# Three edits at the start of a recurrent-attention kernel: V stores behind the Wo load, the first Wq quarter in two pieces, and the order of the second half's context matmuls

## The chip, the cores and the metric

The program runs on 1 core of one Trainium2 chip. Its time is the device time of one execution in microseconds (us). Three runs of the kernel before gave 838.24, 837.37 and 839.92 us, so the median is 838.24 us. Lower is better.

## The reference, cut to what matters

Two layers on 2048 tokens of width 512, in bfloat16. Layer A is attention with a recurrent memory: the tokens are cut into 64 segments of 32; eight memory rows are put ahead of each segment, and the first eight rows of the segment's output are the next segment's memory, so the 64 steps can't run side by side. Layer B is a gated MLP that mixes over all tokens. Layer A takes most of the time, and the edits lie in its first steps and, for the matmul order, in each of them.

```
_A_ref(x, mem0, Wq, Wk, Wv, Wo):           # 32 heads of 128
    mem = mem0                              # 8 rows
    for s in range(64):
        h = concatenate([mem, x[32 rows of segment s]])        # 40 rows
        q, k, v = h @ Wq, h @ Wk, h @ Wv                       # per head
        p = softmax(mask(q @ k.T * scale))
        o = (p @ v) @ Wo                                       # summed over heads
        mem = o[:8];  outs.append(o[8:])
h  = x + _A_ref(_layernorm(x), ...)
h2 = h + _B_ref(_layernorm(h), ...)         # gelu, layernorm, w_sp mixing, w_out
```

## The kernel before, in words

**Tiles and stages.** All of Wq, Wk, Wv and Wo (4 MB each) stay on chip in one buffer, `f_arena`. The start loads them in quarters of 1 MB (eight heads) and meanwhile projects rows that don't depend on the memory: the last eight rows of each segment, transposed into `hTe` in four chunks of 16 segments (`ck`). Then come 64 steps `s`. A step projects 32 of its 40 rows (`QK`, line 539; `V_half`, line 645), multiplies queries by keys (`S_half`, lines 590 and 596), takes the softmax, multiplies by the values (`PV_half`, lines 670 and 676), evacuates that context to `cT` (lines 694 and 696), applies Wo (`Wo`, line 708) and makes the next memory (`mem_out`, line 735). Heads 0 to 15 are half `b = 0`, heads 16 to 31 half `b = 1`. In the gaps of a step stand matmuls that the chain doesn't need at once, among them V projections of later chunks (`vx_mm`, line 476).

**V projections of the extra rows.** `vx_mm(ck, n)` makes the `n`th of eight pieces of a chunk. `vx_evac` (lines 480 to 505) copies the piece from PSUM to a staging buffer and stores it to DRAM (`vext_d`, DMA issue on line 494), from where `load_vx` (line 511) fetches one segment's values. Chunk 0 is staged in `part`; other chunks go through the two halves of `Vs` in turn (`vcnt`), so an evacuation has to wait until the store that last read its half has landed. For chunk 0 and `n >= 2` the stores of the later segments are put off: `vrest[0]` holds six stores of segments 2 to 5, `vrest[1]` those of segments 6 to 15.

**Order.** `Emitter.add` lists instructions in program order, engine by engine, and derives the semaphore waits from the tokens read and written. Every engine runs its own list in order. SP and ACT issue DMAs in their lists, and an issue that has to wait holds up all that stands behind it. DMAs of SP and ACT take the semaphores `fdma0` to `fdma35` in turn.

**Around the change.** Wq's quarters come first, the upper two 128-row blocks of each on SP's queue and the lower two on ACT's (`load_w`, line 313). SP goes on with x, Wv, Wk and Wo (line 922). The start's Q and K groups of four heads (`qkx_full`, line 449) begin with heads 0 to 3. Step 0 makes pieces (1, 0) and (1, 1) of V in the middle, (1, 2) and (2, 0) behind its context; (2, 0) is evacuated by ACT (line 488) behind `mem_out`, ahead of ACT's mask copy (line 574) and ACT's evacuations of the next step's Q and K (line 550). Behind the evacuation of (1, 1), step 0 lists the six held `vrest[0]` stores with a wait for Wo's last quarter, a transposing read of `w_sp` (`wT_read(0, 0)`, line 851) and a load of x rows (`load_xe(3, 1)`, line 303).

**Context banks.** The four 32-row groups `c` of a half write four PSUM banks. For half 1 the order of `c` is 1, 2, 3, 0 in the first 16 matmuls and 2, 1, 3, 0 in the last four; the Wo matmuls and the evacuations go 0, 2, 1, 3.

Of the kernel before, what the change touches and what calls it, by code (L numbers as in the profile page):

```python
# [169 lines left out]
def fast_path(nc, st, keep, flags, A_x, A_mem0, A_Wq, A_Wk, A_Wv, A_Wo, A_seg_len, B_w_in, B_w_sp, B_b_sp, B_w_out, out):  # L170
# [3 lines left out]
    DH = A_Wq.shape[2]  # L174
# [21 lines left out]
    em = Emitter(n_dma_sems=40)  # L196

    def sb(name, shape, dt):
        return st.enter_context(nc.sbuf_tensor("f_" + name, shape, dt))
# [19 lines left out]
    hTe = sb("hTe", [128, NCK, DC, 128], BF)  # L219
# [12 lines left out]
    partx = sb("partx", [128, 512], BF)  # L232
# [38 lines left out]
    def PB(b):  # L271
        return ("ps", b)

    def sp(fn, **k):
        return em.add("sp", fn, dma=True, **k)

    def pe(fn, **k):
        return em.add("pe", fn, **k)

    def act(fn, **k):  # L280
        return em.add("act", fn, **k)

    def dve(fn, **k):
        return em.add("dve", fn, **k)
# [13 lines left out]
    def xbuf(j):  # L298
        return (xn[:, j, :], [("xn", j)]) if j < 2 else (part[:, j, :], [("part", j, 0), ("part", j, 1)])

    def load_xe(ck, j, queue="sp"):
        t, tok = xbuf(j)
        em.add(queue, lambda e: e.dma_start(t, xe[CK * ck:CK * ck + CK, XM:SEG, :]), dma=True, writes=tok)

    def load_w(mi, hq, queues=("sp",)):
        parts = len(queues)
        n = DC // parts
        wd, ws = ((A_Wq, w_q), (A_Wk, w_k), (A_Wv, w_v))[mi]
        wr = wd.rearrange("(dc p) h e -> p dc (h e)", p=128)
        cols = slice(hq * 8 * DH, (hq + 1) * 8 * DH)  # L310
        for k in range(parts):
            tok = ("W", mi, hq) if k == 0 else ("W", mi, hq, k)
            em.add(queues[k], lambda e, k=k: e.dma_start(ws[:, k * n:(k + 1) * n, cols], wr[:, k * n:(k + 1) * n, cols]), dma=True, writes=[tok])  # L313
            em.mark_const(tok)

    load_xe(0, 0)
    load_xe(1, 1, "act")
    for hq in range(4):
        load_w(0, hq, ("sp", "act"))
        if hq == 1:  # L320
            act(lambda e: e.preload_act_table_set("natural_log_exp_and_others"))
    load_x(0, 4)
# [120 lines left out]
    def qkx_full(ck, i, bank):  # L443
        mi, h0 = i // 8, 4 * (i % 8)
        ws = (w_q, w_k)[mi]
        for hh in range(4):
            h = h0 + hh
            for dc in range(DC):
                pe(lambda e, h=h, dc=dc, hh=hh: e.matmul(ps[:, bank, hh * 128:(hh + 1) * 128], lhsT=ws[:, dc, h * DH:(h + 1) * DH],
                                                         rhs=hTe[:, ck, dc, :], start=(dc == 0), stop=(dc == DC - 1)),  # L450
                   reads=[("hTe", ck), ("W", mi, h // 8) if mi or dc < 2 else ("W", mi, h // 8, 1)], writes=[PB(bank)])

    def qkx_full_evac(ck, i, bank, eng):
        mi, h0 = i // 8, 4 * (i % 8)
# [25 lines left out]
    def vx_evac(ck, n, bank, eng="act", queue="sp"):  # L480
        if ck == 0:
            t, tok = part[:, n, :], [("part", n, 0), ("part", n, 1)]
        else:
            j = vcnt[0] % 2
            vcnt[0] += 1
            t, tok = Vs[:, j, :], [("Vs", j)]
        if eng == "act":
            act(lambda e: e.activation(out=t, in_=ps[:, bank, :], func=ACT.Copy, scale=VSC), reads=[PB(bank)], writes=tok)
        else:
            dve(lambda e: e.tensor_scalar(out=t, in0=ps[:, bank, :], scalar1=VSC, scalar2=None, op0=ALU.mult), reads=[PB(bank)], writes=tok)  # L490
        def store(i0, i1, ks, queue="sp", after=()):
            r = slice(8 * i0, 8 * i1)
            dst = vext_d[ck, n, r, :, :].rearrange("p r e -> p (r e)")
            em.add(queue, lambda e: e.dma_start(dst, t[r, :]), dma=True, reads=tok, writes=[("vext", ck, n, k) for k in ks], after=after)

        if ck:
            store(0, CK, (0,), queue)
        else:
            store(0, 2, (0,), queue)
            if n < 2:  # L500
                store(2, CK, (1, 2))
            else:
                vrest[0].append(lambda after=(): store(2, 6, (1,), after=after))
                vrest[1].append(lambda: store(6, CK, (2,)))

    vcnt, vrest = [0], ([], [])
# [149 lines left out]
        else:  # L656
            dve(lambda e: e.tensor_scalar(out=dst, in0=src, scalar1=VSC, scalar2=None, op0=ALU.mult), reads=[PB(bank)], writes=tok)  # L657

    PVO = ((0, 1, 2, 3), (1, 2, 3, 0))

    def pv_bank(b, c):
        return CB if (b, c) == (1, 0) else PVB[c]

    def PV_half(s, b):
        xb = s % NVX
        for g in range(4):
            for c in PVO[b]:
                q = slice(32 * c, 32 * c + 32)
                c0 = 160 * b + 40 * g
                pe(lambda e, q=q, c=c, g=g, c0=c0: e.matmul(  # L670
                    ps[:, pv_bank(b, c), c0:c0 + 40], lhsT=V_sb[q, b, g * 128:(g + 1) * 128], rhs=E_sb[q, b, 0:160].rearrange("p (a g t) -> p a g t", a=5, t=8)[:, :, g, :],
                    start=(g == 0), stop=False, skip_group_check=True, tile_position=(32 * c, 0)),
                    reads=[("V", b, g), ("E", b)], writes=[PB(pv_bank(b, c))])
        for c in (PVO[0], (2, 1, 3, 0))[b]:
            q = slice(32 * c, 32 * c + 32)
            pe(lambda e, q=q, c=c: e.matmul(  # L676
                ps[:, pv_bank(b, c), 160 * b:160 * b + 160].rearrange("p (g q) -> p g q", q=40)[:, :, 0:16], lhsT=Vx[q, xb, b, :],
                rhs=E_sb[q, b, 160:224].rearrange("p (g q) -> p g q", q=16),
                start=False, stop=True, skip_group_check=True, tile_position=(32 * c, 0)),
                reads=[("Vx", xb), ("Ex", b)], writes=[PB(pv_bank(b, c))])  # L680
# [73 lines left out]
    def behind():  # L754
        return [em.by_eng["pe"][-1]]
# [93 lines left out]
    def wT_read(i, k):  # L849
        r = slice(8 * k, 8 * k + 8)  # L850
        sp(lambda e: e.dma_start_transpose(out=wst[:, r, :], in_=B_w_sp[i * 64:(i + 1) * 64, 1024 * k:1024 * k + 1024]),
           writes=[("wst", k)], after=behind())
# [36 lines left out]
    def start_x(ck, i):  # L889
        start_group(qkx_full, qkx_full_evac, ck, i)  # L890
# [5 lines left out]
    for hq in (0, 2, 1, 3):  # L896
        load_w(2, hq)
# [23 lines left out]
    for hq in range(4):  # L921
        sp(lambda e, hq=hq: e.dma_start(w_o[:, 8 * hq:8 * hq + 8, :], wor[:, 8 * hq:8 * hq + 8, :]), writes=[("Wo", hq)])  # L922
        em.mark_const(("Wo", hq))


    class Gap:
# [88 lines left out]
    for s in range(NSEG):  # L1015
# [3 lines left out]
            w2_load()  # L1019
        if j4 == 3 and rb > 0:  # L1020
            px_load(rb - 1)
        if s > 0:
            wT_read(s // 2, s % 2)

        def qk_piece(pi):
            QK(s, QKP[pi], range(2 if pi < 2 else 1 if pi == 2 and s else 0, DC))
# [67 lines left out]
        sm_rcp(1)  # L1094
        if s == 0:
            vx_evac(1, 1, 5, "act")
            for f in vrest[0]:
                f([em.last_w[("Wo", 3)]])
            wT_read(0, 0)
            load_xe(3, 1)  # L1100
        if s > 0:
            v_second()
        if j4 == 1:
# [210 lines left out]
    for i, rb in enumerate(order):  # L1314
# [8 lines left out]
        if i == 1:  # L1323
            pe(lambda e: e.matmul(ps[:, CB, :], lhsT=Sc[:], rhs=partx[:], start=True, stop=True),
               reads=["partx", "Sc"], writes=[PB(CB)])
# [52 lines left out]
    for tb in range(NTB):  # L1378
        for fb in range(len(ACC) if tb == 0 else 0, FB):
            bank = 5 + fb % 3 if tb == 0 else (tb * FB + fb) % 2  # L1380
# [777 lines left out]
```

## Time and profile before

| | us |
|---|---|
| median of three runs | 838.24 |
| the profiled execution, whole | 840.62 |
| its span, first to last instruction | 838.90 |
| TensorE (PE) busy in the span | 824.4 (98%) |
| ScalarE (ACT) busy | 514.2 (61%) |
| VectorE (DVE) busy | 475.9 (57%) |
| GpSimd (POOL) busy | 145.0 (17%) |

A span counts from the first instruction of the program to the last; the 1.72 us between it and the execution's time lie around it. All times inside a profile are from the span's start. PE is the matmul array, PEld its weight load, SPq the queue of SyncE, which issues most DMAs. A row of the timeline gives the start, the length, engine, source line, operation, output and inputs, and how many instructions are merged; brackets give the idle time before it and what ended that. A row of the waits gives the engine and line that waited, what released it, the total, the number of waits and the longest.

### The profile page before, as it was taken

The page shows a single profiled execution, that of the slowest core. Times are in us where ns is not written, and L with a number is a line of the kernel's source. Part 1 is how long each engine was busy: PE and PEld are TensorE (multiplying, and loading weights), DVE is VectorE, ACT ScalarE, POOL GpSimd, SP SyncE. Part 2 cuts the span into 40 slices and gives each one's busy share as a digit, 9 for nine tenths or more (in the row PEclk, how much of TensorE's full clock was granted, in tenths as well). Part 3 has the DMA queues.
Part 4 walks back from the last instruction along what each step waited for, and adds up shares of the span by engine and source line. Part 5 has one row for each costly group of instructions (what it writes and reads, how often), then busy time and mean ns, then how long its engine had stood idle before and what let it go on. Part 6 is the DMA issues. An engine that isn't in the chain of part 4 may idle for free.

```text
span 838.9 us, 48365 instructions
## 1 busy us (share of the span) xinstructions
PE 824.4 (98%) x21963; PEld 484.4 (58%) x21963; DVE 475.9 (57%) x1221; ACT 514.2 (61%) x1549; POOL 145.0 (17%) x412
## 2 busy tenths in 40 slices
PE   7999999999999999999999999999999999999998
PEld 7755565656566555655566656555665554444443
DVE  3546565656566555666556556565655576653344
ACT  2467777777777777777777777676666676300000
POOL 5202111121121111112211121111111123200000
PEclk9999999999999999999999999999999999999999
DMA  9975222122222222222212122333343278223101
GB/s 313 386 214 108 69 60 68 49 68 60 61 63 58 65 60 65 63 73 58 67 50 72 48 70 72 103 85 85 78 83 84 73 253 260 90 101 103 42 13 48
DMA packets 107652, 80.54 MB, mean 96 GB/s; under 512 B 49672, under 2 KB 97040, under 8 KB 107440
## 3 DMA queue, kind: packets, MB, share of 16 engines
q1 hardware_dynamic: 105712, 74.82, 30.8%
q8 instruction: 174, 2.85, 1.5%
q10 hardware_dynamic: 1504, 2.36, 0.9%
q14 instruction: 38, 0.31, 0.1%
q0 software_dynamic: 224, 0.20, 0.1%
HBM read 43.72 MB, written 23.13 MB: 80 GB/s over the span
## 4 chain that ended last, share of the span: by engine, by line
PE 92%; SPq 5%; DMA 1%; issue 0%; ACT 0%; DVE 0%; POOL 0%; POOLq 0%
PE f_ps L539 27%; PE f_ps L708 14%; PE f_ps L645 13%; PE f_ps L1266 12%; PE f_ps L426 4%; PE f_ps L764 4%; SPq L313 3%; PE f_ps L1360 3%; PE f_ps L1259 3%; PE f_ps L670 3%; PE f_ps L476 2%; PE f_ps L830 2%; PE f_ps L590 1%; DMA f_arena<-in_A_Wo_dram 1%; SPq L922 1%; PE f_ps L1226 1%
## 5 line engine op out<-in xcount | busy, mean ns | idle before, releaser
L539 PE MATMUL f_ps<-f_arena,f_hT 128*32 128x512 bf16 (+1 forms) x5120 | 238.5, 337 | 0.4
L539 PEld LDWEIGHTS f_ps<-f_arena,f_hT 128*32 128x32 bf16 x5120 | 124.4, 96 | 89.0 <-ACT f_hT L738 20.0
L550 ACT ACTIVATE f_Tst<-f_ps 128x512 bf16<-128x512 f32 (+2 forms) x320 | 143.4, 510 | 36.1 <-PE f_ps L539 28.5
L645 PE MATMUL f_ps<-f_arena,f_hT 128*32 128x512 bf16 x2048 | 139.8, 379 | 0.0
L708 PE MATMUL f_ps<-f_arena,f_cT 128*32 128x256 bf16 x4096 | 130.1, 273 | 2.2 <-DMA f_arena<-in_A_Wo_dram 1.3
L635 POOL TENSOR_TENSOR f_E_sb<-f_R_sb,f_E_sb 128x64 bf16<-128x64 f32 x128 | 47.5, 371 | 411.0 <-ACT f_R_sb L627 411.0
L708 PEld LDWEIGHTS f_ps<-f_arena,f_cT 128*32 128x32 bf16 x4096 | 97.0, 96 | 27.5 <-ACT f_cT L694 17.3
L558 DVE STREAM_TRANSPOSE f_QT<-f_Tst 128x256 uint32<-128x256 uint32 x128 | 57.1, 446 | 93.2 <-ACT f_Tst L550 93.2
L657 DVE TENSOR_SCALAR f_V_sb<-f_ps 128x512 bf16<-128x512 f32 (+1 forms) x128 | 71.4, 558 | 52.4 <-PE f_ps L645 52.4
L1266 PE MATMUL f_ps<-f_arena 128*128 128x512 bf16 x448 | 100.5, 379 | 0.0
L1266 PEld LDWEIGHTS f_ps<-f_arena 128*128 128x128 bf16 x448 | 43.7, 98 | 52.9 <-issue 0.3
L694 ACT ACTIVATE f_cT<-f_ps 128x160 bf16<-128x160 f32 (+1 forms) x192 | 55.6, 329 | 26.0 <-PE f_ps L676 25.4
L696 DVE TENSOR_SCALAR f_cT<-f_ps 128x256 bf16<-128x256 f32 x128 | 48.4, 420 | 36.7 <-PE f_ps L676 36.7
L604 ACT ACTIVATE f_E_sb<-f_ps 128x224 bf16<-128x224 f32 x128 | 46.3, 362 | 36.6 <-PE f_ps L616 35.4
L727 ACT ACTIVATE f_part<-f_ps 128x256 bf16<-128x256 f32 x128 | 49.3, 385 | 20.6 <-PE f_ps L708 16.1
L558 DVE STREAM_TRANSPOSE f_KT<-f_Tst 128x256 uint32<-128x256 uint32 (+2 forms) x192 | 58.4, 330 | 4.5 <-ACT f_Tst L550 1.8
L645 PEld LDWEIGHTS f_ps<-f_arena,f_hT 128*32 128x32 bf16 x2048 | 47.1, 95 | 19.8 <-issue 0.4
L738 ACT ACTIVATE f_hT<-f_ps 128x16 bf16<-128x16 f32 x126 | 23.3, 185 | 45.8 <-PE f_ps L735 45.8
L1272 DVE TENSOR_TENSOR f_arena<-f_ps,f_arena 128x512 f32<-128x512 f32 x28 | 19.3, 690 | 52.5 <-PE f_ps L1266 50.5
L627 ACT ACTIVATE f_R_sb<-f_R_sb 128x160 f32<-128x160 f32 x128 | 43.3, 338 | 4.0
L576 DVE CAST f_ps<-f_mask 128x224 f32<-128x224 bf16 x80 | 29.9, 373 | 26.9 <-ACT f_hT L406 24.5
L426 PE MATMUL f_ps<-f_arena,f_hTe 128*32 128x512 bf16 x640 | 41.9, 379 | 0.0
(127 smaller groups left out, 1157.8 us busy)
## 6 DMA issues: line engine op xcount, KB each, us to landing
wT_d<-f_wst SPq DMA_DIRECT2D x64, 128.0 KB
f_arena<-wT_d SPq DMA_DIRECT2D x32, 256.0 KB
f_arena<-in_A_Wv_dram SPq DMA_DIRECT2D x4, 1024.0 KB
f_arena<-in_A_Wk_dram SPq DMA_DIRECT2D x4, 1024.0 KB
f_arena<-in_A_Wo_dram SPq DMA_DIRECT2D x4, 1024.0 KB
f_Vx<-vext_d SPq DMA_DIRECT2D x62, 64.0 KB
vext_d<-f_Vs SPq DMA_DIRECT2D x24, 128.0 KB
zp_d<-f_Vs SPq DMA_DIRECT2D x20, 112.0 KB
```

Source lines behind the costliest of these rows:

```text
L426: pe(lambda e, c=c, rhs=rhs: e.matmul(ps[32 * c:32 * c + 32, bank, :], lhsT=hTe[:, ck, dc, 32 * sg:32 * sg + 32], rhs=rhs, start=(dc == 0) ...
L539: pe(lambda e, dc=dc, c=c, rhs=rhs: e.matmul(ps[32 * c:32 * c + 32, bank, 0:32 * nh], lhsT=hT[:, sl, dc, :], rhs=rhs, start=(dc == 0), sto ...
L550: act(lambda e: e.activation(out=st_.rearrange("p (hp i r) -> p hp i r", i=32, r=2), in_=ps[:, bank, 0:64 * np_].rearrange("p (hp r i) -> ...
L558: dve(lambda e: e.transpose(out=dst, in_=src), reads=tok, writes=[(nm, b, k) for k in halves(b, p0, np_)])
L635: pool(lambda e: e.tensor_tensor(out=ev, in0=rv, in1=ev, op=ALU.mult), reads=[("R", b), ("Ex", b)], writes=[("Ex", b)])
L645: pe(lambda e, dc=dc, c=c, c0=c0: e.matmul(ps[32 * c:32 * c + 32, bank, 0:w], lhsT=hT[:, sl, dc, :], rhs=w_v[:, dc, c0:c0 + w], start=(dc ...
L657: dve(lambda e: e.tensor_scalar(out=dst, in0=src, scalar1=VSC, scalar2=None, op0=ALU.mult), reads=[PB(bank)], writes=tok)
L694: act(lambda e: e.activation(out=dst, in_=src, func=ACT.Copy, scale=UNSC), reads=[PB(bank)], writes=tok)
L696: dve(lambda e: e.tensor_scalar(out=dst, in0=src, scalar1=UNSC, scalar2=None, op0=ALU.mult), reads=[PB(bank)], writes=tok)
L708: pe(lambda e, h=h, g=g, i=i, b=b, c=c: e.matmul(ps[32 * g:32 * g + 32, bank, 0:d1 - d0], lhsT=cTh[:, i, 8:40], rhs=w_o[:, h, d0:d1], star ...
L727: act(lambda e: e.activation(out=part[:, s % 8, d0:d1], in_=ps[:, bank, 0:d1 - d0], func=ACT.Copy), reads=[PB(bank)], writes=[("part", s % ...
L1266: pe(lambda e: e.matmul(ps[:, bank, 0:TB], lhsT=z2[:, sc, fb * 128:(fb + 1) * 128], rhs=wTb[tb % 2][:, :, sc, :], start=first, stop=last), ...
```

## The change

1. `vx_evac` stages piece (1, 0) in `partx`, a buffer that is otherwise first used in step 6. The later pieces move by one in the turns of `Vs`: (1, 1) and (2, 0) now use one half, (1, 2) and (1, 3) the other.
2. The six `vrest[0]` stores are listed right behind the Wo loads, and `wT_read(0, 0)` and `load_xe(3, 1)` at the start of step 0. So on SP's queue they stand ahead of the stores of (1, 0) and (1, 1).
3. The first quarter of Wq is loaded in two pieces of four heads, on each of its two queues, with tokens of their own; the first Q group waits for the first piece alone.
4. In half 1 the context matmuls go through `c` as 0, 2, 1, 3.

```
-    def load_w(mi, hq, queues=("sp",)):
+    def load_w(mi, hq, queues=("sp",), u=None):
...
-        cols = slice(hq * 8 * DH, (hq + 1) * 8 * DH)
+        cols = slice(hq * 8 * DH, (hq + 1) * 8 * DH) if u is None else slice(4 * u * DH, 4 * (u + 1) * DH)
         for k in range(parts):
-            tok = ("W", mi, hq) if k == 0 else ("W", mi, hq, k)
+            tok = ("Wh", k) if u == 0 else ("W", mi, hq) if k == 0 else ("W", mi, hq, k)
...
     for hq in range(4):
-        load_w(0, hq, ("sp", "act"))
+        for u in (None,) if hq else (0, 1):
+            load_w(0, hq, ("sp", "act"), u)
...
-                   reads=[("hTe", ck), ("W", mi, h // 8) if mi or dc < 2 else ("W", mi, h // 8, 1)], writes=[PB(bank)])
+                   reads=[("hTe", ck), ("Wh", dc // 2) if i == 0 else ("W", mi, h // 8) if mi or dc < 2 else ("W", mi, h // 8, 1)], writes=[PB(bank)])
...
             t, tok = part[:, n, :], [("part", n, 0), ("part", n, 1)]
+        elif (ck, n) == (1, 0):
+            t, tok = partx[:], ["partx"]
         else:
...
-    PVO = ((0, 1, 2, 3), (1, 2, 3, 0))
+    PVO = ((0, 1, 2, 3), (0, 2, 1, 3))
...
-        for c in (PVO[0], (2, 1, 3, 0))[b]:
+        for c in PVO[b]:
...
         em.mark_const(("Wo", hq))
+    for f in vrest[0]:
+        f([em.last_w[("Wo", 3)]])
...
-        if s > 0:
-            wT_read(s // 2, s % 2)
+        wT_read(s // 2, s % 2)
+        if s == 0:
+            load_xe(3, 1)
...
             vx_evac(1, 1, 5, "act")
-            for f in vrest[0]:
-                f([em.last_w[("Wo", 3)]])
-            wT_read(0, 0)
-            load_xe(3, 1)
```

SP's list from the Wo loads on, before the change. `f_part` stores are the held `vrest[0]` ones, `f_Vs` the stores of the V pieces, in the order (1, 0), (1, 1), and further down (1, 2), (2, 0).

```order
L922 DMA f_arena<-in_A_Wo_dram 128x8x512 x4
L494 DMA vext_d<-f_Vs 128x512 [waits fs_dve]
L494 DMA vext_d<-f_Vs 128x512 [waits fs_act]
L494 DMA vext_d<-f_part 32x512 [waits fdma31]
L494 DMA vext_d<-f_part 32x512 x5
L851 DMA_TRANSPOSE f_wst<-in_B_w_sp_dram 128x8x64
L303 DMA f_xn<-in_A_x_dram 128x1x512
L295 DMA f_xn<-in_A_x_dram 128x512
L856 DMA wT_d<-f_wst 128x512 [waits fdma4,fs_pe]
```

The same place of the changed kernel; `f_partx` is the store of (1, 0), the `f_Vs` behind it that of (1, 1).

```order
L925 DMA f_arena<-in_A_Wo_dram 128x8x512 x4
L497 DMA vext_d<-f_part 32x512 [waits fs_dve,fdma33]
L497 DMA vext_d<-f_part 32x512 [waits fs_act]
L497 DMA vext_d<-f_part 32x512 [waits fs_dve]
L497 DMA vext_d<-f_part 32x512 [waits fs_act]
L497 DMA vext_d<-f_part 32x512 [waits fs_dve]
L497 DMA vext_d<-f_part 32x512 [waits fs_act]
L854 DMA_TRANSPOSE f_wst<-in_B_w_sp_dram 128x8x64 [waits fs_pe]
L303 DMA f_xn<-in_A_x_dram 128x1x512
L497 DMA vext_d<-f_partx 128x512 [waits fs_dve]
L497 DMA vext_d<-f_Vs 128x512 [waits fs_act]
```

Both V stores moved from ahead of the wait for Wo's last quarter (`fdma31` before, `fdma33` now) to eight and nine places behind it. Counted from the waiting DMA, `fdma33`, in turns of 36, the store of (1, 1) is the tenth next and has the semaphore `fdma7`.

ACT's list at the end of step 0 and the start of step 1, before the change: the two halves of the next memory, the evacuation of V piece (2, 0) to `f_Vs`, the mask copy, then the first Q and K evacuations.

```order
L738 ACTIVATE f_hT<-f_ps 128x2x8 [waits fs_pe]
L488 ACTIVATE f_Vs<-f_ps 128x512 [waits fdma33]
L574 ACTIVATE f_ps<-f_mask 128x224 [waits fs_dve]
L550 ACTIVATE f_Tst<-f_ps 128x512 [waits fs_pe] x2
L550 ACTIVATE f_Tst<-f_ps 128x512 [waits fs_dve,fs_pe]
```

The same place of the changed kernel.

```order
L741 ACTIVATE f_hT<-f_ps 128x2x8 [waits fs_pe]
L491 ACTIVATE f_Vs<-f_ps 128x512 [waits fdma7]
L577 ACTIVATE f_ps<-f_mask 128x224 [waits fs_dve]
L553 ACTIVATE f_Tst<-f_ps 128x512 [waits fs_pe] x2
L553 ACTIVATE f_Tst<-f_ps 128x512 [waits fs_dve,fs_pe]
```

The order on ACT is unchanged. In both kernels the evacuation of (2, 0) waits for the store of (1, 1), `fdma33` before and `fdma7` now; what moved is the place of that store on SP's queue.

## The prediction

> **What bounds the kernel now.** I read the page first, for the engine and the chain of work that ended last.
>
> ```profile
> PE 824.4 (98%) x21963; PEld 484.4 (58%) x21963; DVE 475.9 (57%) x1221; ACT 514.2 (61%) x1549; POOL 145.0 (17%) x412
> PE 92%; SPq 5%; DMA 1%; issue 0%; ACT 0%; DVE 0%; POOL 0%; POOLq 0%
> ```
>
> PE carries 92% of the chain, SP's queue and DMA 6%. So whatever holds PE up costs its full length. Where SP and DMA take over is told by the chain in order of time, in its first 62 us (start, length, what).
>
> ```profile
> 27.06 2.98 SPq L313
> ...
> 32.62 6.74 SPq L922
> ...
> 42.84 12.13 DMA f_arena<-in_A_Wo_dram
> 54.97 0.04 issue
> 55.01 1.38 PE f_ps L708 x44
> ```
>
> The chain of the start is one row of weight loads, which ends when Wo's last quarter lands at 54.97. PE joins only there. So until 55.0 an earlier PE is worth nothing unless that quarter lands earlier too; from there on, PE's own time and every stall of PE count. The waits of the first 60 us, PE's and one of DVE's and ACT's:
>
> ```profile
> PE f_ps L449 <- DMA f_arena<-in_A_Wq_dram: 3.3, 1, 3.3
> PE f_ps L708 <- DMA f_arena<-in_A_Wo_dram: 1.3, 1, 1.3
> DVE f_Vs L490 <- DMA vext_d<-f_Vs: 1.6, 1, 1.6
> ACT f_hTe L411 <- PE f_ps L387: 8.1, 2, 5.3
> ```
>
> The edits of the start touch the first three rows; the fourth is a cover that is used below.
>
> **Edit by edit: Wq's first quarter.** With half of the quarter's bytes to wait for, PE can start its Q groups up to half of 3.3 us earlier, 1.7 us. By the chain this isn't worth anything by itself: PE would stand 1.3 + 1.7 = 3.0 us before Wo's last quarter instead of 1.3. ACT issues one DMA more; it waits 8.1 us for PE in this stretch, which hides it, and without that cover it would be one issue of about 0.5 us (SP's shortest rows of line 313 in the chain are that long). What counts is whether the load gets slower: its rows in DRAM are now 512 elements, 1 KB, instead of 2 KB. Wk is read in 2 KB rows and Wo in 1 KB rows, and the windows show both (last column GB/s):
>
> ```profile
> 30.00:35.00 5.00, 5.00 (x100) 2.60 (x96) 2.07 (x3) 1.57 (x4) 1.60 (x3) 1.00 1.05 388
> 45.00:50.00 5.00, 5.00 (x130) 3.88 (x131) 2.11 (x6) 2.77 (x8) 0.00 (x0) 1.00 1.08 322
> ```
>
> One quarter of 1.05 MB takes 2.7 us at 388 and 3.3 us at 322 GB/s, so Wo's end moves by 0 to +0.55 us. I take the middle, **+0.3**, since the first microseconds don't reach the 388 anyway.
>
> **The two V stores.** They leave the time before Wo's end. SP's queue there:
>
> ```profile
> 50.15 2.17 SPq L494 DMA_DIRECT2D vext_d<-f_Vs  x2
> 54.99 3.31 SPq L494 DMA_DIRECT2D vext_d<-f_part  x6
> 58.34 1.33 SPq L851 DMA_TRANSPOSE f_wst<-in_B_w_sp_dram  x1
> 59.71 0.57 SPq L303 DMA_DIRECT2D f_xn<-in_A_x_dram  x1
> 60.33 0.58 SPq L295 DMA_DIRECT2D f_xn<-in_A_x_dram  x1
> 61.34 0.34 SPq L856 DMA_DIRECT2D wT_d<-f_wst  x1
> ```
>
> Did they slow Wo? They carry 0.26 MB, 0.8 us at 322 GB/s, which bounds the gain. But DVE's evacuation of (1, 2), which waited for the first of them, started only at 55.36:
>
> ```profile
> 55.36 0.69 DVE L490 TENSOR_SCALAR f_Vs<-f_ps 128x512 bf16<-128x512 f32 x1 [1.59 <-DMA vext_d<-f_Vs]
> 59.18 0.45 DVE L558 STREAM_TRANSPOSE f_QT<-f_Tst 128x256 uint32<-128x256 uint32 x1 [3.13 <-ACT f_Tst L550]
> 59.67 0.45 DVE L558 STREAM_TRANSPOSE f_KT<-f_Tst 128x256 uint32<-128x256 uint32 x1
> ```
>
> So that store, issued at 50.15, landed behind Wo (54.97) and hardly took from it. I take **0**, ends -0.8 and 0. [...]
>
> DVE's 1.59 us of waiting go, since (1, 1) no longer lies on the half that (1, 2) needs. Nobody is behind it: DVE then idles 3.13 us until ACT delivers.
>
> **What is late next.** The held stores now stand on SP's queue behind the wait for Wo and behind the six `f_part` stores, the transposing read and the x load. These eight issues are the same as before and in the same order, so SP reaches the store of (1, 0) where it now issues the x load of line 295, at 60.33, and with 0.34 for that (the row at 61.34) and 0.04 between, the store of (1, 1) at **60.71**. ACT's list at the end of step 0:
>
> ```profile
> 57.49 0.18 ACT L738 ACTIVATE f_hT<-f_ps 128x16 bf16<-128x16 f32 x1 [0.37 <-PE f_ps L735]
> 57.57 0.59 ACT L488 ACTIVATE f_Vs<-f_ps 128x512 bf16<-128x512 f32 x1
> 58.05 0.37 ACT L574 ACTIVATE f_ps<-f_mask 128x224 f32<-128x224 bf16 x1
> 58.55 2.32 ACT L550 ACTIVATE f_Tst<-f_ps 128x512 bf16<-128x512 f32 x5
> ```
>
> L488 at 57.57 is piece (2, 0). It writes the half of `Vs` that the store of (1, 1) reads, so it waits for that landing (`fdma7` in ACT's list). Before, that store had been issued by 52.4 and was 5 us old by then; now it isn't even issued for another 3.1 us. From the issue to the landing no row shows such a store on an idle queue. The bounds are 0, and 5.3 us, the median of POOL's stores beside full queues, in the list of DMA issues:
>
> ```profile
> vext_d<-f_part POOLq DMA_DIRECT2D x4, 16.0 KB, 5.3
> ```
>
> SP's own waits between 60 and 62 us have the nearest row:
>
> ```profile
> SPq L158 <- DMA f_wst<-in_B_w_sp_dram: 0.3, 1, 0.3
> ```
>
> It is the transposing read on SP's own queue: issued at 58.34, and SP waited for it ahead of the write at 61.34, 3.0 us later. I take 2.9, so the store lands at 63.6 and ACT is held from 57.57 until then, **6.0** (bounds 3.1 and 8.4). [...]
>
> Behind L488 on ACT stand the mask copy and the five evacuations of step 1's Q and K. For these wait DVE's transposes, and for those PE:
>
> ```profile
> 57.25 3.20 PE L539 MATMUL f_ps<-f_arena,f_hT 128*32 128x512 bf16 x72
> 60.28 0.27 PE L590 MATMUL f_ps<-f_QT,f_KT 128*32 128x40 bf16 x16
> 60.41 1.04 PE L645 MATMUL f_ps<-f_arena,f_hT 128*32 128x512 bf16 x16
> ```
>
> PE's Q and K matmuls cover ACT until 60.28; then come the scores (L590), which need the transposed keys, ready at 59.67 + 0.45 = 60.12. The cover is 0.16 us. So PE stands still for 6.0 - 0.16, about **5.9** (3.0 to 8.3), and the V matmuls of L645 stand behind the scores in PE's list and can't fill the gap.
>
> **The clock after such a stall.** The start shows what an idle PE does to its clock (columns: length, then busy of PE, PEld, DVE, ACT, POOL, then granted clock):
>
> ```profile
> 4.18:7.60 3.42, 1.81 (x24) 1.41 (x22) 2.30 (x6) 0.60 (x1) 2.14 (x6) 1.00 0.96 302
> 7.60:11.01 3.41, 0.36 (x7) 0.39 (x8) 0.00 (x0) 0.00 (x0) 2.39 (x13) 1.00 1.04 374
> 11.01:14.42 3.41, 3.41 (x36) 3.41 (x34) 0.89 (x2) 0.62 (x2) 2.38 (x12) 0.50 1.05 398
> ```
>
> A stretch of 3.41 us with 0.36 busy is followed by one at half clock, one with 1.81 busy is not. A stall of 5.9 covers at least most of one such stretch. The half clock partly falls into the stall itself; if the stall begins with a stretch, 0.9 us of work runs at half clock (loss 0.45) and the next stretch, 27% busy of the one before, may be halved too (0.45 + 1.7); if it begins in the middle of one, 2.6 us run at half clock (1.3). I take **+1.3**, ends 0.45 and 2.2. [...]
>
> **The order of half 1.** The 16 and 4 matmuls are the same, only their turn differs. The Wo matmuls of two steps in the chain:
>
> ```profile
> 164.12 1.53 PE f_ps L708 x56
> 173.92 1.57 PE f_ps L708 x56
> ```
>
> Of 56 matmuls, some steps lose 0.04 us. If the order took that from about half of the 63 later steps, it would give 1.3 us; a turn later for one group costs at most 0.01 in each, 0.6. ACT evacuates `c = 0` of half 0 first and is busy when half 1 ends, so I take **0**.
>
> **Sum.** 0.3 + 0 + 5.9 + 1.3 + 0 = +7.5 us. The profiled execution took 840.62 (span 838.90 and 1.72 around it) and would take 848.1; it lies 2.38 above the median of 838.24, which is what runs are measured by, so the forecast is 838.24 + 7.5 = **845.7**.
>
> **Rivals.**
> - *Faster: Wo lands early and the wait on ACT never forms.* Both PE waits of the start would go, 1.3 + 1.7, giving 838.24 - 3.0 = 835.2. It decides at 57.57: the store of (1, 1) must land within 2.6 us of Wo's end. Against it: the eight issues ahead of it alone take 5.3 us. For it: only that Wo's end and PE's matmuls behind it would move together. Chance 0.04.
> - *The change doesn't do what it says.* If the wait of ACT were for a store that is long done, only the load's +0.3 would be left, 838.5. ACT's list speaks against it. Chance 0.04.
> - *A second stall.* SP itself waits for the evacuation of (2, 0), to store it, and behind it stand the next transposing read and the load of `Vx` for step 2. If PE had to wait for that load as well, some 4 us more, 849.7. Against it: PE is late by as much as SP, so the distance stays. Chance 0.07.
>
> **How the numbers follow.** My forecast has 0.85. Its own ends are the landing's: with 0 for it, 838.24 + 0.3 + 3.0 + 0.45 = 842.0; with 5.3, 838.24 + 0.3 + 8.3 + 2.2 = 849.0. The other unknowns are smaller and hardly all at one end, so I give 842.0 to 849.0; it leaves out the two rivals below, the second stall, and little of my own case. About 0.3%, 2.5 us, is what a measurement of this kernel can tell from no change. Faster by more has the first rival's 0.04, within it the second's 0.04, slower 0.92.
>
> **What would show it.** In the profile of the changed kernel: a wait of about 6 us of ACT's `f_Vs` evacuation for a `vext_d` store; an idle PE of nearly the same length just before the scores of step 1; a stretch at half clock behind it; Wo's last quarter near 55.3 and PE waiting for it longer than 1.3; DVE's 1.6 gone; steps from the third on as long as before. It is wrong if ACT's evacuation starts near 57.6, or if Wo lands microseconds earlier.

## The result, and the profile after

The changed kernel takes 848.97 us (median of 6 runs, 846.16 to 852.63). The kernel before, run beside it, takes 837.75 us (6 runs, 837.31 to 839.92). The ratio is 1.013, with a 95% interval of 1.0102 to 1.0158: the change makes the kernel 11.2 us slower, where 7.5 us had been forecast. The median lies 0.03 us inside the upper end of the forecast's 842.0 to 849.0. In a second group of runs (`again`, below) the ratio was 1.0096, 1.0063 to 1.0129, which is 7.8 us by medians. The profiled execution of the changed kernel took 848.11 us, with a span of 846.3; that is 7.49 us more than the profiled execution of before. All numbers from inside the kernel below compare these two.

Two lines of the page first: busy time by engine, and the engines of the chain that ended last.

```profile
PE 827.1 (98%) x21963; PEld 494.2 (58%) x21963; DVE 475.2 (56%) x1221; ACT 510.0 (60%) x1549; POOL 144.5 (17%) x412
PE 91%; DMA 4%; SPq 2%; issue 1%; ACT 1%; DVE 0%; ACTq 0%
```

The same 21963 matmuls are on record, busy for 2.7 us more. PE is 98% busy in both kernels, so the page alone hides a loss of 7 us; one has to look at the place. Four of the waits of the first 90 us, in the changed kernel:

```profile
ACT f_Vs L491 <- DMA vext_d<-f_Vs: 5.4, 1, 5.4
PE f_ps L593 <- DVE f_KT L561: 5.0, 1, 5.0
PE f_ps L711 <- DMA f_arena<-in_A_Wo_dram: 1.3, 1, 1.3
PE f_ps L450 <- DMA f_arena<-in_A_Wq_dram: 0.6, 1, 0.6
```

The first two rows are new. PE's wait for Wo is what it was, 1.3, and that for Wq has shrunk from 3.3 to 0.6. DVE's wait of 1.6 for a `vext_d` store has gone. SP's queue shows why ACT waits (start, length, line, what):

```profile
54.65 3.39 SPq L497 DMA_DIRECT2D vext_d<-f_part  x6
58.09 1.32 SPq L854 DMA_TRANSPOSE f_wst<-in_B_w_sp_dram  x1
59.46 0.57 SPq L303 DMA_DIRECT2D f_xn<-in_A_x_dram  x1
60.08 0.58 SPq L497 DMA_DIRECT2D vext_d<-f_partx  x1
60.71 0.43 SPq L497 DMA_DIRECT2D vext_d<-f_Vs  x1
```

The store of piece (1, 1) is issued at 60.71, the very time that the prediction had given. ACT's timeline at the end of step 0:

```profile
57.15 0.18 ACT L741 ACTIVATE f_hT<-f_ps 128x16 bf16<-128x16 f32 x1 [0.37 <-PE f_ps L738]
62.73 0.60 ACT L491 ACTIVATE f_Vs<-f_ps 128x512 bf16<-128x512 f32 x1 [5.39 <-DMA vext_d<-f_Vs]
63.22 0.36 ACT L577 ACTIVATE f_ps<-f_mask 128x224 f32<-128x224 bf16 x1
63.50 2.31 ACT L553 ACTIVATE f_Tst<-f_ps 128x512 bf16<-128x512 f32 x5
```

ACT could have gone on at 57.34 and stood until 62.73, 2.0 us after the store's issue. The mask copy and the Q and K evacuations of step 1 stood behind it. PE, in the start and at the same place:

```profile
7.92 1.91 PE L450 MATMUL f_ps<-f_hTe,f_arena 128*128 128x128 bf16 x16
...
30.60 3.64 PE L477 MATMUL f_ps<-f_arena,f_hTe 128*32 128x512 bf16 x64 [1.46 <-issue]
...
54.68 1.39 PE L711 MATMUL f_ps<-f_arena,f_cT 128*32 128x256 bf16 x44 [1.27 <-DMA f_arena<-in_A_Wo_dram]
...
56.92 3.20 PE L542 MATMUL f_ps<-f_arena,f_hT 128*32 128x512 bf16 x72
65.11 0.30 PE L593 MATMUL f_ps<-f_QT,f_KT 128*32 128x40 bf16 x16 [4.99 <-DVE f_KT L561]
...
65.31 1.90 PE L648 MATMUL f_ps<-f_arena,f_hT 128*32 128x512 bf16 x16
```

PE ends its Q and K matmuls at 60.12 and stands 4.99 us for the transposed keys. Then the 16 V matmuls take 1.90 instead of 1.04. The last column but two of the windows says why, the granted clock:

```profile
58.40:61.81 3.41, 1.72 (x48) 1.02 (x40) 0.00 (x0) 0.00 (x0) 0.00 (x0) 1.00 0.45 126
61.81:65.22 3.41, 0.11 (x16) 0.11 (x20) 1.06 (x3) 2.40 (x6) 0.00 (x0) 1.00 0.69 220
65.22:68.63 3.41, 3.41 (x76) 1.54 (x76) 1.60 (x5) 1.73 (x7) 0.17 (x1) 0.50 0.25 62
68.63:72.04 3.41, 3.41 (x120) 2.15 (x116) 2.15 (x7) 2.10 (x8) 1.21 (x4) 1.00 0.21 62
```

**Where the loss lies.** The two spans differ by 7.42 us. I cut the two traces at the first context matmul of each step (L670 before, L673 after):

```
                                         before    after
start to the context of step 0            52.33    52.05
context of step 0 to context of step 1    11.32    18.09
context of step 1 to context of step 63  611.72   611.34
from there to the end                    163.53   164.83
```

The stretch around the new wait is 6.77 us longer, and the start 0.28 shorter: 6.5 us together. Of that, 4.99 are PE's idle time, and 1.66 lie between the scores of step 1 and its context (5.03 us after, 3.37 before), which is the half clock. The other steps are as long as they were, and the tail, which no edit touches, is 1.3 longer; in the 14 profiles of this study, experiments included, it lies between 163.4 and 166.2, so that isn't the change's. The medians differ by 3.7 us more than the two profiles, since before's profiled execution lies 2.9 above the median of its six runs and after's 0.9 below.

### The profile page after: what moved, and what is told of

Same layout as the page of the kernel before. It is cut to its first block, busy times and chain, and to the rows that moved or that the text cites. A ratio compares the mean times of both kernels' runs of the same rounds, so it can differ in the third digit from the quotient of the medians.

```text
span 846.3 us, 48432 instructions
## 1 busy us (share of the span) xinstructions
PE 827.1 (98%) x21963; PEld 494.2 (58%) x21963; DVE 475.2 (56%) x1221; ACT 510.0 (60%) x1549; POOL 144.5 (17%) x412
## 3 DMA queue, kind: packets, MB, share of 16 engines
q8 instruction: 174, 2.85, 1.4%
## 4 chain that ended last, share of the span: by engine, by line
PE 91%; DMA 4%; SPq 2%; issue 1%; ACT 1%; DVE 0%; ACTq 0%
PE f_ps L542 26%; PE f_ps L711 13%; PE f_ps L648 13%; PE f_ps L1268 11%; PE f_ps L427 4%; PE f_ps L767 4%; PE f_ps L477 3%; PE f_ps L1362 3%; PE f_ps L673 3%; PE f_ps L833 2%; PE f_ps L1261 2%; DMA f_arena<-in_A_Wo_dram 1%; PE f_ps L593 1%; PE f_ps L450 1%; DMA f_arena<-in_A_Wq_dram 1%; PE f_ps L614 1%
## 5 line engine op out<-in xcount | busy, mean ns | idle before, releaser
L542 PEld LDWEIGHTS f_ps<-f_arena,f_hT 128*32 128x32 bf16 x5120 | 129.3, 96 | 87.0 <-ACT f_hT L741 18.2
L648 PE MATMUL f_ps<-f_arena,f_hT 128*32 128x512 bf16 x2048 | 141.5, 382 | 0.1
L711 PEld LDWEIGHTS f_ps<-f_arena,f_cT 128*32 128x32 bf16 x4096 | 99.3, 96 | 23.6 <-ACT f_cT L697 6.5
L697 ACT ACTIVATE f_cT<-f_ps 128x160 bf16<-128x160 f32 (+1 forms) x192 | 51.3, 328 | 24.5 <-PE f_ps L679 24.5
L648 PEld LDWEIGHTS f_ps<-f_arena,f_hT 128*32 128x32 bf16 x2048 | 49.0, 96 | 19.4 <-issue 0.8
L593 PEld LDWEIGHTS f_ps<-f_QT,f_KT 128*32 128x32 bf16 x2048 | 28.6, 95 | 23.5 <-DVE f_KT L561 22.9
```

Source lines behind the costliest of these rows:

```text
L542: pe(lambda e, dc=dc, c=c, rhs=rhs: e.matmul(ps[32 * c:32 * c + 32, bank, 0:32 * nh], lhsT=hT[:, sl, dc, :], rhs=rhs, start=(dc == 0), sto ...
L648: pe(lambda e, dc=dc, c=c, c0=c0: e.matmul(ps[32 * c:32 * c + 32, bank, 0:w], lhsT=hT[:, sl, dc, :], rhs=w_v[:, dc, c0:c0 + w], start=(dc ...
L697: act(lambda e: e.activation(out=dst, in_=src, func=ACT.Copy, scale=UNSC), reads=[PB(bank)], writes=tok)
L711: pe(lambda e, h=h, g=g, i=i, b=b, c=c: e.matmul(ps[32 * g:32 * g + 32, bank, 0:d1 - d0], lhsT=cTh[:, i, 8:40], rhs=w_o[:, h, d0:d1], star ...
```

## The experiments

The **theory** is that the loss is the wait of ACT for the held store of (1, 1), the PE stall that follows and the half clock behind that. The **rivals**: the new order of half 1's context matmuls costs something in each step, or the split load of Wq delays what comes behind. The runs fall into three groups; each group ran on one chip beside the kernel before, so the ratios are within a group and the microseconds of different groups aren't compared.

| group | run | what it has | median us (range, runs) | before us | ratio (95%) |
|---|---|---|---|---|---|
| 1 | again | the change, all four edits | 849.64 (844.52 to 852.37, 6) | 841.83 | 1.0096 (1.0063 to 1.0129) |
| 1 | own_buffer | all, and a buffer of its own for (1, 1) | 843.58 (838.71 to 848.93, 12) | 841.83 | 1.0021 (0.9997 to 1.0044) |
| 1 | half_hold | all, but two issues fewer ahead of the V stores | 844.95 (843.39 to 851.08, 12) | 841.83 | 1.0046 (1.0024 to 1.0069) |
| 1 | pe_fill | all, and 66 extra matmuls in the stall | 853.64 (848.33 to 855.22, 6) | 841.83 | 1.0125 (1.0089 to 1.0162) |
| 2 | stores_only | edits 1 and 2 | 845.82 (840.89 to 853.42, 10) | 840.22 | 1.0079 (1.0049 to 1.0108) |
| 2 | no_hold | edits 1, 3 and 4 | 843.98 (841.61 to 846.85, 6) | 840.22 | 1.0070 (1.0045 to 1.0095) |
| 2 | wq_only | edit 3 | 840.96 (839.08 to 845.04, 12) | 840.22 | 1.0020 (0.9999 to 1.0041) |
| 2 | pv_only | edit 4 | 843.36 (841.87 to 845.6, 8) | 840.22 | 1.0052 (1.0032 to 1.0071) |
| 3 | aa | none, before against itself | 841.38 (837.12 to 846.44, 12) | 840.14 | 1.0010 (0.9985 to 1.0035) |
| 3 | pv_again | edit 4 once more | 843.45 (840.33 to 845.26, 12) | 840.14 | 1.0037 (1.0015 to 1.0059) |
| 3 | old_order | edits 1, 2 and 3 | 847.8 (844.83 to 852.62, 7) | 840.14 | 1.0092 (1.0051 to 1.0133) |
| 3 | own_old | edits 1 and 2, and the buffer of its own | 841.48 (836.93 to 847.56, 12) | 840.14 | 1.0003 (0.9971 to 1.0035) |

The ratio on record is not the quotient of the two medians: `no_hold` has 0.70% by its ratio and 0.45% by medians, `pv_only` 0.52% and 0.37%. Percentages below are the ratio's, microseconds the medians'.

**The change once more** (`again`, no edit).

> The changed kernel once more, as the reference for the three runs beside it. Theory (ACT waits for the store of V piece (1, 1), PE idles about 5 us ahead of step 1's scores, and then a stretch at half clock): 846 to 853 again, so some 8 to 15 us over the kernel before, with a wide spread since the idle time meets the clock's stretches at another place in each run.

It is 0.96% slower, 7.8 us, just under the 8 to 15 expected. Its profile has the same wait, ACT 5.5 and PE 5.1 us.

**The wait taken away** (`own_buffer`). Against the changed kernel, piece (1, 1) gets a staging buffer that is free at that time, so that (2, 0) has no store to wait for:

```
         elif (ck, n) == (1, 0):
             t, tok = partx[:], ["partx"]
+        elif (ck, n) == (1, 1):
+            t, tok = xo[:, 1, :], [("xo", 1)]
```

> As the changed kernel, but V piece (1, 1) is staged in a buffer of its own (half of xo, unused until step 12), so that the evacuation of (2, 0) on ACT waits for no store. SP's queue keeps the order of the changed kernel. Theory: ACT's wait of 5.4 us and PE's of 5.0 go, step 0 takes 11.0 to 11.3 us again and the time is 837.0 to 838.5. Rival one (SP's new order makes a later load late): about 849 as the changed kernel. Rival two (the order of the context matmuls or Wq's pieces cost it): about 849 as well.

The median falls by 6.1 us against `again`, to 0.2% above before. ACT's evacuation of (2, 0) and the next one of the same kind, one step later:

```profile
57.09 0.59 ACT L493 ACTIVATE f_Vs<-f_ps 128x512 bf16<-128x512 f32 x1
...
68.65 0.60 ACT L493 ACTIVATE f_Vs<-f_ps 128x512 bf16<-128x512 f32 x1 [1.07 <-DMA vext_d<-f_Vs]
```

The first one no longer waits; the second now does, 1.07 us. SP's queue, DVE and PE there:

```profile
60.85 2.35 SPq L499 DMA_DIRECT2D vext_d<-f_xo  x1
...
64.23 0.94 SPq L499 DMA_DIRECT2D vext_d<-f_Vs  x2
```

```profile
68.32 0.69 DVE L495 TENSOR_SCALAR f_Vs<-f_ps 128x512 bf16<-128x512 f32 x1 [3.63 <-DMA vext_d<-f_Vs]
...
71.17 0.44 DVE L563 STREAM_TRANSPOSE f_QT<-f_Tst 128x256 uint32<-128x256 uint32 x1
```

```profile
71.99 0.28 PE L595 MATMUL f_ps<-f_QT,f_KT 128*32 128x40 bf16 x16 [1.63 <-DVE f_KT L563]
```

Step 0 is back to 11.57 us (18.09 with the change, 17.11 in `again`), and step 1 has a new stall of 1.63. SP is still late with the stores, so the next reuses of the halves of `Vs` wait: ACT's for 1.07 us and, longer, DVE's for 3.63. DVE's transposes, which PE then waits for, start only at 71.17, when ACT had been done with the first evacuations of Q and K since 70.50. In this profile the one issue of `f_xo` took 2.35 us; in `own_old`, below, it took 0.43, DVE waited 0.70 and PE's scores not at all. The time was expected within 0.75 us of before, which stood at 837.75 then, and came out 1.75 over the before of its group, so that part of the expectation was missed. Against `again`, the wait and its clock are worth 6.1 us here, by medians.

**A shorter wait** (`half_hold`). Against the changed kernel, the transposing read and the x load go back behind the V stores:

```
-        wT_read(s // 2, s % 2)
-        if s == 0:
-            load_xe(3, 1)
+        if s > 0:
+            wT_read(s // 2, s % 2)
...
             vx_evac(1, 1, 5, "act")
+            wT_read(0, 0)
+            load_xe(3, 1)
```

> As the changed kernel, but the transposing read and the x load go back behind the two V stores, so that the store of (1, 1) is issued some 2.2 us earlier, still behind Wo and the six held stores. Theory: ACT waits 3.0 to 3.4 instead of 5.4 us, PE idles 2.6 to 3.0, the clock is halved in few runs, time 840.0 to 842.5. Rivals: no dependence on this place, about 849.

One row each of SP's, ACT's and PE's timelines:

```profile
58.61 0.43 SPq L497 DMA_DIRECT2D vext_d<-f_Vs  x1
```

```profile
60.46 0.60 ACT L491 ACTIVATE f_Vs<-f_ps 128x512 bf16<-128x512 f32 x1 [3.51 <-DMA vext_d<-f_Vs]
```

```profile
62.84 0.28 PE L593 MATMUL f_ps<-f_QT,f_KT 128*32 128x40 bf16 x16 [3.11 <-DVE f_KT L561]
```

The store is issued 2.1 us earlier than in the changed kernel's profile, ACT waits 1.9 less and PE 1.9 less, and no stretch behind it is at half clock. Both waits came out just above what had been expected; the median is 3.1 us over before, 4.7 under `again`. The loss follows the wait. This profile also has the stall without the half clock: from the scores of step 1 to its context it takes 3.46 us, where the eight profiles without a stall there have 3.37 or 3.38, and those with a stall and a halved stretch more:

```
scores of step 1 to its context, us
no stall (8 profiles)            3.37 to 3.38
stall of 3.11, full clock        3.46  half_hold
stall, one halved stretch        4.53  again    4.62  stores_only    4.90  pe_fill    5.03  the change
stall, two halved stretches      6.22  old_order
```

So one halved stretch cost 1.2 to 1.7 us, and two cost 2.8.

**The clock by itself** (`pe_fill`). To keep PE busy through the stall, 66 matmuls on a constant tile stand ahead of step 1's scores:

```
+        if s == 1:
+            for _ in range(66):
+                pe(lambda e: e.matmul(ps[:, WXB, 0:160], lhsT=onesrc[:, 0:128], rhs=onesrc[:, :], start=True, stop=True),
+                   reads=["onesrc"], writes=[PB(WXB)])
         S_half(s, 0)
```

> As the changed kernel, with 66 matmuls on ones (128x160, written to an unused PSUM bank, no part of the output) in step 1 ahead of the scores, where PE idles; they take about 4.6 us. Theory: ACT waits as long as in the changed kernel, but PE is busy, so its clock isn't halved: 1.3 to 3.5 us less than the changed kernel, 845.5 to 847.5, and a spread under 2 us. Rival: the half clock falls into waits and costs nothing, the time is that of the changed kernel or above.

This failed. PE's rows, and ACT's:

```profile
60.35 4.74 PE L1068 MATMUL f_ps<-f_onesrc 128*128 128x160 bf16 x66
...
67.23 0.33 PE L593 MATMUL f_ps<-f_QT,f_KT 128*32 128x40 bf16 x16 [2.14 <-DVE f_KT L561]
```

```profile
64.85 0.60 ACT L491 ACTIVATE f_Vs<-f_ps 128x512 bf16<-128x512 f32 x1 [7.21 <-DMA vext_d<-f_Vs]
```

In this profile the store (issued at 60.99) landed 3.9 us after its issue instead of 2.0, so PE had 2.14 us left to wait; behind a stretch of 3.41 us with PE busy for 1.43, the granted clock was 0.50 from 67.08 to 70.49 all the same. The kernel came out slower than the change, though the mean granted clock of its six runs is higher (0.9977 against 0.9945 in `again`). What made it slower isn't known beyond the longer landing in this one profile, so the price of the clock can't be taken from this run. What there is for that price is the comparison of profiles above.

**The stores alone** (`stores_only`): edits 1 and 2 on the kernel before.

```
+        elif (ck, n) == (1, 0):
+            t, tok = partx[:], ["partx"]
...
+    for f in vrest[0]:
+        f([em.last_w[("Wo", 3)]])
...
```

> The kernel before with the first two edits alone (partx for V piece (1, 0), the held stores, the transposing read and the x load ahead of the two V stores); Wq in one piece and the old matmul order. Theory: the whole loss of the changed kernel, 0.9 to 1.4% over the kernel before, with ACT's wait of 5 to 7 us for the store of (1, 1). Rival (Wq's pieces or the order of the context matmuls carry part of it): clearly less than the changed kernel's loss.

```profile
62.05 0.60 ACT L490 ACTIVATE f_Vs<-f_ps 128x512 bf16<-128x512 f32 x1 [4.60 <-DMA vext_d<-f_Vs]
```

The wait is there, and 5.6 us by medians with it. So the wait comes from the stores, not from the other two edits. The loss, 0.79%, is below the 0.9 to 1.4% that had been expected, though its interval reaches 1.08: this run alone doesn't say that the other edits carry nothing.

**All but the held stores** (`no_hold`): edit 2 is taken back from the changed kernel, `vrest[0]`, the transposing read and the x load stand where they stood before.

> The changed kernel without the second edit: SP's order is that of the kernel before, the other three edits stay. Theory: ACT doesn't wait, step 0 as before, time within 0.25% of the kernel before on either side; Wo's last quarter lands within 0.6 us of 54.97. Rival (the other edits cost it): over 0.5% slower.

It missed: not within 0.25% of before, but 0.70% above it (3.8 us by medians). ACT's wait is gone, as it should be, but PE waits 2.1 us for Wo in this profile instead of 1.3, and a half clock follows:

```profile
51.26:54.68 3.42, 1.34 (x66) 0.77 (x63) 1.48 (x4) 1.02 (x5) 0.24 (x1) 1.00 0.54 182
54.68:58.09 3.41, 3.41 (x68) 2.41 (x72) 0.00 (x0) 0.91 (x3) 0.00 (x0) 0.50 0.17 46
```

In its profile, step 0 takes 13.65 us, 2.3 more than before, after a start that is 1.1 shorter. This is one profile; the runs that tell edits 3 and 4 apart come next.

**Wq's split alone** (`wq_only`): the `load_w` lines and the reads of the first Q group of the diff.

> The kernel before with the third edit alone, Wq's first quarter in two pieces by heads. Theory: PE's first wait falls from 3.3 to under 1.7 us, Wo's last quarter lands between 0.3 earlier and 0.6 us later, PE waits longer for it, and the time stays within 0.15% of the kernel before. Rival (an earlier PE is worth its 1.7 us): 0.2% faster.

Within the measurement of no change: 0.2%, and `aa` reads 0.1%. PE waits 0.6 us for Wq instead of 3.3, and nothing comes of it. Wo's last quarter landed at 53.50 in this profile, 1.5 earlier than in before's, and PE waited 0.9 for it; for both something else had been expected.

**The order alone, twice** (`pv_only`, `pv_again`, the same kernel):

```
-    PVO = ((0, 1, 2, 3), (1, 2, 3, 0))
+    PVO = ((0, 1, 2, 3), (0, 2, 1, 3))
...
-        for c in (PVO[0], (2, 1, 3, 0))[b]:
+        for c in PVO[b]:
```

> The kernel before with the fourth edit alone, the order 0, 2, 1, 3 of the second half's context matmuls. Theory: the 56 Wo matmuls of a step shrink by at most 0.03 us in about half of the steps, so the time is 0 to 1 us less, within 0.15%. Rival (a turn earlier on a bank that ACT has yet to read stalls PE in each step): 0.3% slower or more.

> The kernel of pv_only once more (order of the second half's context matmuls alone). Theory (the order itself costs 2.5 to 4.5 us, though the profile shows no longer step): 0.3 to 0.6% slower again. Rival (the 0.5% was the spread between builds and launches): within 0.25% of the kernel before.

It is slower twice, by 0.52% (0.32 to 0.71) and 0.37% (0.15 to 0.59), 3.1 and 3.3 us by medians; the first expectation, 0 to 1 us faster, was missed. Beside the second one, the **kernel before against itself** read:

> The kernel before, unchanged, run as if it were a change. Any theory: within 0.2% of itself. If it comes out 0.3% or more away, differences of that size between the other kernels carry no weight.

0.10% (-0.15 to 0.35), 1.2 us. If that is taken off, some 2 us are left for the order, but the intervals of `aa` and `pv_again` overlap. The traces don't show a loss. The weight loads of the Wo matmuls, first before, then with the new order (idle ahead of the group, and what ended it):

```profile
L708 PEld LDWEIGHTS f_ps<-f_arena,f_cT 128*32 128x32 bf16 x4096 | 97.0, 96 | 27.5 <-ACT f_cT L694 17.3 <-DMA f_arena<-in_A_Wo_dram 1.5 <-issue 1.1
```

```profile
L708 PEld LDWEIGHTS f_ps<-f_arena,f_cT 128*32 128x32 bf16 x4096 | 99.5, 96 | 22.3 <-ACT f_cT L694 5.9 <-issue 1.5
```

The idle time that `cT` ends is 11.4 us shorter, all idle time of the group 5.2, so the order does something useful there. Steps come in a cycle of four kinds, 9.84, 9.62, 9.68 and 9.90 us long in before where nothing disturbs them; with the new order the first two kinds are 0.03 us shorter and the others are the same. Taken step by step, the medians over the profiles add up to 599.9 us from the context of step 2 to that of step 63 with the old order (before and five experiments), and to 599.0 with the new (eight). The sums of single profiles, from the context of step 1 to that of step 63, are 610.1 to 615.3 us and 612.4 on average with the old order, 609.3 to 615.3 and 612.6 with the new: a spread of 6 us, in which a loss of 2 could hide. The granted clock doesn't explain a loss either: its mean over the runs is 0.9972 and 0.9974 with the new order alone, 0.9964 and 0.9965 for before beside them.

**All but the order** (`old_order`): the changed kernel with the two `PVO` lines of before.

> The changed kernel with the fourth edit undone, so edits one to three. If the order costs by itself: 2.5 to 4.5 us less than the changed kernel, 0.5 to 0.9% over the kernel before. If it doesn't: 0.9 to 1.4% over the kernel before, as the changed kernel in its two measurements.

0.92%, against 0.96% of `again` in another group and 1.3% of the first measurement. That is on the side of an order that costs nothing, but the interval, 0.51 to 1.33%, holds both expectations. Its profile has the wait (ACT 5.9, PE 5.5) and two stretches at half clock:

```profile
60.60:64.01 3.41, 0.00 (x0) 0.00 (x0) 0.09 (x1) 1.49 (x4) 0.00 (x0) 1.00 0.78 231
64.01:67.42 3.41, 2.52 (x68) 1.35 (x72) 2.23 (x7) 1.93 (x6) 0.00 (x0) 0.50 0.46 127
67.42:70.84 3.42, 3.42 (x44) 1.30 (x36) 1.33 (x4) 1.74 (x6) 1.14 (x3) 0.50 0.18 52
```

**The held stores without the wait** (`own_old`): edits 1 and 2 with the two `xo` lines of `own_buffer`, and nothing else.

> Edits one and two with V piece (1, 1) in a buffer of its own, the old matmul order and Wq in one piece. ACT doesn't wait for the store. If the order costs by itself: 0.1 to 0.4% faster than the kernel before, since the same with the new order and Wq's pieces was 0.2% slower. If it doesn't: within 0.25%.

It equals before, 1.0003 (0.9971 to 1.0035; 1.3 us over by medians), and is 6.3 us under `old_order`, which has the wait and the Wq split besides. ACT has no wait there and step 0 takes 10.88 us. Within some 3 us either way, holding the stores back costs nothing once nobody waits for them, and brings nothing either.

## Why the prediction was right, and where not

The sign and the mechanism were right, and shown: with the wait the loss is there (`stores_only`, `old_order`, `again`), with a buffer of its own it goes in both pairs (6.1 and 6.3 us by medians), and a shorter wait costs less (`half_hold`). The steps, one by one:

- **Wo's last quarter**, +0.3: it landed at 54.64, 0.33 earlier than before, and PE waited 1.27 for it. One pair of profiles can't tell such a size: over the 14 profiles the store that waits for Wo is issued between 52.57 and 55.16, at 54.42 on average in the eight with Wq's pieces and at 54.03 in the six without. Whether the 1 KB rows delay it stays open.
- **Wq's first quarter**, nothing by itself: right (`wq_only`). PE began the Q groups at 7.92 instead of 10.65. At 25.50 it was 2.24 us ahead of before; 1.46 of that went in a pause ahead of the next V projections, at 30.60, for which the profile names no cause (they read later parts of Wv; that a load of these was late is a guess, and not shown). At the context of step 0, 0.28 were left. The argument behind it, that PE joins only at Wo's landing, was read from one profile. In five of the six profiles with Wq in one piece, one or two stretches at half clock stand in the first 17 us, in the eight with two pieces none, and in three of those five (`aa`, `pv_only`, `stores_only`) PE came to Wo too late to wait for it. The mean granted clock of `wq_only`'s runs is 0.9992, that of before beside it 0.9964. So edit 3 does save clock at the start, and still no time that shows in the whole.
- **The V stores took nothing from Wo**, 0: `own_old` equals before, so no gain is hidden there, as far as its interval of some 3 us either way goes.
- **The store's issue at 60.71**: exact in this profile, and by luck. SP reached the store of (1, 0) at 60.08 and not at 60.33, since Wo had landed earlier, and that issue took 0.58 and not 0.34; the two errors cancel. In the other profiles of SP's same order, with the wait, the store is issued at 59.92 to 61.15. **Its landing 2.9 us later**: mis-sized, 2.0. In six profiles with the wait it took 1.85 to 2.13 us in five, and 3.9 in `pe_fill`.
- **PE's stall of 5.9**: 4.99; the landing's error of 0.9 accounts for it.
- **The clock, +1.3, ends 0.45 and 2.2**: 1.66 in the profile, one stretch at half clock as described, and 1.2 to 1.7 in the four profiles with one. The two stretches of `old_order` cost 2.8, beyond the end.
- **The order of half 1, 0, with ends of -1.3 and 0.6**: this is the step that failed, if one did. Two measurements say about 3 us, 2 after `aa` is taken off, and the end of 0.6, for which I had put 0.01 us a step by estimate with no row that shows it, was too near. For it stands a further pair in one group, `no_hold` (with it) 0.50% above `wq_only` (without it), 3.0 us by medians, though these differ by edit 1 too, and by a halved stretch behind Wo that `no_hold`'s profile has and `wq_only`'s has not. Against it stand `old_order` and `own_old`, whose intervals are too wide to decide, and the step times of the profiles. Whether there is such a loss, and where it would come from, stays open.
- **The rivals**: there was no gain, and the change did what it says. The second stall, on the load of `Vx`, didn't form in the changed kernel, where PE is as late as SP, as argued. With PE early and SP late (`own_buffer`) a stall of 1.6 us came, but by another way: DVE waited for a store of `Vs`, and PE for DVE.

By the profile, the mechanism cost 6.5 us where 7.5 had been summed up. By the medians the loss was 11.2, with an interval of 8.5 to 13.2, and 8 in the second group. The 4.7 between are, by arithmetic, the 3.7 by which the two profiled executions stand differently to their medians and the 1.3 of the tail, less 0.4 in the steps. The clocks on record show what most executions of the changed kernel had and its profile had not. Two of the six, the profiled one among them, have a mean granted clock of 0.998, in the profiled one with one stretch of 3.41 us at half clock in its span of 846.3; they take 847.1 us on average. The other four have 0.994 or 0.995, by estimate 8 to 10 us at a clock of 0.50, and take 849.9. In `again` the profiled run has 0.998 and takes 844.52, the fastest of its six; the other five have 0.993 to 0.995 and take 849.8. So both profiles caught the mild case, and the term of the sum that was too small for most executions is most likely the clock. Where their further halved stretches lie, no trace shows; in before's profile 1.9 us of half clock lie at the program's end, so not all of it is behind the stall. The open step above may be part of the difference too. That 848.97 still fell into the stated range, by 0.03 us, is luck.

## What to carry to other kernels

When a store is put off, look for the next writer of its buffer, not only for the reader of its data: here ACT's evacuation waited 5.4 us for a store whose data nobody needed yet, and with one more staging buffer the same two edits cost nothing that could be measured. The issue time of the moved store could be worked out from the durations on its queue, to within the 0.8 us by which it differs from profile to profile; its landing and the clock behind the stall were the uncertain terms. A single profile can show the mild case: the granted clock of every run tells how the others went. An edit that is meant to work in each of 63 steps by hundredths of a microsecond needs the kernel measured against itself first, since one round of runs here moved by 0.1% with no edit at all.

## What the runs showed of the hardware that was not expected

**PE's busy time ahead of the halved stretches.** In the first 100 us of the 14 profiles, I took PE's busy time in the 3.41 us ahead of each stretch at half clock:

```
first halved after (PE busy of 3.41 us)       0.00, 0.00, 0.00, 0.11, 0.35, 0.95, 0.95, 0.96, 1.33, 1.43, 1.51
not halved, lowest cases on the same grid     1.62, 1.66, 1.72, 1.80
halved stretch, next one halved too           1.99, 2.12, 2.39, 2.52
halved stretch, next one at full clock        2.51, 2.70, and from 3.10 up
```

The last of the first row is from the start of `own_old` (the same columns as above, 3.41 us each):

```profile
4.75:8.16 3.41, 1.51 (x20) 1.11 (x17) 2.05 (x6) 0.60 (x1) 2.32 (x7) 1.00 1.03 390
8.16:11.57 3.41, 3.10 (x30) 3.13 (x31) 0.89 (x2) 0.60 (x1) 2.38 (x12) 0.50 1.05 395
```

And the lowest case that wasn't halved, behind the stall of 3.11 us in `half_hold`, which two stretches shared:

```profile
57.64:61.05 3.41, 2.08 (x56) 1.20 (x48) 0.00 (x0) 0.59 (x2) 0.00 (x0) 1.00 0.42 127
61.05:64.46 3.41, 1.62 (x72) 1.00 (x76) 2.28 (x7) 2.78 (x9) 0.00 (x0) 1.00 0.70 217
64.46:67.88 3.42, 3.42 (x116) 1.95 (x112) 2.21 (x8) 2.73 (x11) 1.38 (x4) 1.00 0.32 82
```

In these profiles, then, a stretch at full clock with PE busy for 1.51 us or less was followed by a halved one, and one with 1.62 or more was not. Behind a halved stretch the next was halved again after up to 2.52 us, and at full clock after 2.51 in one case, 2.70 in another, and from 3.10 up. In eight of the eleven cases of the first row PE had worked in the stretch ahead, for 0.11 to 1.51 us. The 2.1 us that PE waited for Wo in `no_hold` lay in one stretch, with 1.34 us busy, and the next was halved; the 3.11 of `half_hold` lay in two, with 2.08 and 1.62 busy, and the stretch behind each was at full clock.

**PE's short stops without a releaser stood on a grid in these traces.** Undisturbed steps of a kind are alike within some 0.01 us, but each profile has 5 to 15 stops of 0.15 to 1.8 us between 75 and 685 us, most of them put down to "issue", and 1.3 to 5.8 us in all, beside the spread of 6 us between the sums of single profiles above. Counted in matmuls from the start of the program, most of them stand whole multiples of 127.8 apart with the old order, of 127.65 with the new:

```
before        3926, 8401, 12875, 17605, 18245, 20162    differences / 127.86: 35.0, 35.0, 37.0, 5.0, 15.0
matmul 8401   in before, stores_only, wq_only, own_old   (old order)
matmul 14517  in after, again, own_buffer, half_hold, no_hold, pv_only, pv_again   (new order)
```

The page's line on DMA queues has 174 packets of instructions (q8), 2.85 MB, 16.4 KB each. In the 14 traces each of the 106 stops put down to "issue" ends 1.2 to 1.6 us after the end of a packet of that queue, while these packets come 3.9 us apart on average. The new order's traces have 63 more waits in PE's list, 155 sequencer instructions instead of 92, and the slightly shorter distance. What holds PE up at these places, no run shows, and the stops don't explain the open step: per profile they come to 2.9 us on average with either order.
